# Loading q and k in runs of four tokens (1 KB), with heads 0-3 on partitions 0-63 and heads 4-7 on partitions 64-127

## The chip, the cores and the metric

The kernel runs on one core of one Trainium2 chip. The metric is device time in microseconds of one execution; a kernel's time is the median of its fast executions. The profile's span runs from the first to the last recorded instruction, so it is a little shorter than the device time (302.3 us where 304.1 us was timed for the same run). Some executions fall into a slower state with a lower TensorE clock; they are marked and left out of every comparison.

## The reference, cut to what matters

The reference is attention inside chunks of 64 tokens, followed by a bilinear feed-forward block on the result. Batch is 8, heads 8, sequence 576, head size 64, all in fp32:

```python
q_c = q.reshape(B, H, nc, chunk, D)                 # chunk = 64, the same for k and v
attn = softmax(np.matmul(q_c, k_c.transpose(0, 1, 2, 4, 3)) / sqrt(D))
out = np.matmul(attn, v_c)
x = out.transpose(0, 2, 1, 3).reshape(4608, 512)    # tokens x (heads * head size)
return (x @ w_a) * (x @ w_b) @ w_out                # w_a, w_b: 512 x 1536, w_out: 1536 x 512
```

## The kernel before

It works on units of 256 tokens (18 units). A unit that crosses from one batch into the next is loaded in two pieces. For the first units (q of units 0 to 5, k of units 0 to 4) q and k are transposed on TensorE; later ones are transposed by DMA. The change touches only those first units. These are the parts concerned:

```python
# load: two tokens to a partition, so each of the 8 heads brings a run of 512 B
st = st_pool.tile([128, H, 2, D], FP32, name="st")
for r, b, s, m in pieces(U):
    nc.sync.dma_start(
        out=st[r // 2:(r + m) // 2].rearrange("p h i d -> p h (i d)"),
        in_=src[b, :, s:s + m, :].rearrange("h (p i) d -> p h (i d)", i=2),
    )
staged[n, U] = st.rearrange("p h i d -> p i h d")
...
# transpose_pe: 8 transposes into PSUM, then two copies that interleave the tokens again
for i in range(2):
    for m in range(NKT):
        nc.tensor.transpose(tp[i][:, m, :],
            src[:, i, 2 * m:2 * m + 2, :].rearrange("p j d -> p (j d)"), identity)
dst = qkt[U][:, w].rearrange("c g m (p i) -> c i m g p", i=2)
for i in range(2):
    on_dve = i == 0 if U == 0 else w == 0 or U == 1
    cp = nc.vector.tensor_copy if on_dve else nc.scalar.copy
    cp(out=dst[:, i], in_=tp[i].rearrange("c m (g p) -> c m g p", g=2))
```

Partition p holds tokens 2p and 2p+1, so a transpose of "token i of every partition" yields every second token, and the copy out of PSUM writes every second bf16 element (a step of two). And in unit 1, on which the head of the kernel ends, all four copies are VectorE's.

The softmax here doesn't subtract the row's maximum and nothing guards it: scores larger than these inputs give would overflow.

## Time and profile before

| | before |
|---|---|
| median (three runs, then four with one more beside the changed kernel) | 303.82 us, then 303.66 us |
| span of the profiled run | 302.3 us |
| TensorE busy | 292.4 us, 97% |
| VectorE, ScalarE, GpSimd busy | 69%, 65%, 64% |
| start of the first real matmul of the feed-forward block | 17.65 us |

The busy rows show tenths of busy time in 40 equal slices of the span. These are the four copies of unit 1 in the kernel before, from VectorE's instructions in order of time (start, duration, engine, line, operation, output and input; in brackets the idle time before it and what ended it):

```profile
9.42 0.73 DVE L240 COPY qkt<-pq 128x512 bf16<-128x512 bf16 x1 [1.22 <-PE pq L231]
10.05 0.71 DVE L240 COPY qkt<-pt 128x512 bf16<-128x512 bf16 x1
10.93 0.73 DVE L240 COPY qkt<-pb 128x512 bf16<-128x512 bf16 x1 [0.17 <-PE pb L231]
11.55 0.71 DVE L240 COPY qkt<-pa 128x512 bf16<-128x512 bf16 x1
```

Two of them had to wait for transposes (the brackets of 1.22 and 0.17). From the first copy's start to the scores at 12.32 is 2.90 us. VectorE is busy in nearly all of this stretch, so a copy that is much longer shows up in full.

### The profile page before, as it was taken

The numbers are of one execution on the slowest core, as the hardware profiler recorded it, in microseconds if no ns is written. First come the engines' busy times: TensorE is split into PE (matmuls) and PEld (weight loads), VectorE is DVE, ScalarE is ACT, GpSimd is POOL, SyncE is SP. The second block draws the span as 40 slices with busy tenths as digits, with TensorE's granted clock in tenths as the row PEclk, the third lists the DMA queues.
The fourth block names the chain that finished last, engine by engine and source line by source line (L and its number), as shares of the span: only waits on it lengthen the run. The fifth ranks groups of instructions, "written<-read, shape, count | busy, mean of one in ns | idle before, by whom it ended". The sixth has DMA issues, their size and how long they took to land.

```text
span 302.3 us, 8608 instructions
## 1 busy us (share of the span) xinstructions
PE 292.4 (97%) x3527; PEld 231.9 (77%) x3527; DVE 210.0 (69%) x343; ACT 196.5 (65%) x355; POOL 193.3 (64%) x180
## 2 busy tenths in 40 slices
PE   6799999999999999999999999999999999999995
PEld 2344367866588888888888888888888888888884
DVE  3456575878767696769676966796679667965773
ACT  2643567348387768776867687768776876566532
POOL 0665758995999698808880888178817901780660
PEclk9999999999999999999999999999999999999999
DMA  7999999999999999896959395958721001100024
GB/s 222 307 382 284 283 336 345 242 217 210 219 239 262 213 242 276 188 210 181 208 122 245 129 205 132 210 163 198 123 87 72 2 2 69 73 0 3 2 98 179
DMA packets 141127, 54.29 MB, mean 180 GB/s; under 512 B 117152, under 2 KB 135200, under 8 KB 141088
## 3 DMA queue, kind: packets, MB, share of 16 engines
q1 hardware_dynamic: 140944, 53.69, 69.9%
q8 instruction: 27, 0.44, 0.6%
q14 instruction: 12, 0.10, 0.1%
q10 hardware_dynamic: 144, 0.07, 0.1%
HBM read 37.75 MB, written 9.44 MB: 156 GB/s over the span
## 4 chain that ended last, share of the span: by engine, by line
PE 83%; DMA 5%; SPq 4%; DVE 3%; POOL 1%; ACT 1%; issue 1%; DVEq 0%; ACTq 0%; POOLq 0%
PE pb L440 19%; PE pc L440 12%; PE pa L440 12%; PE po L578 12%; PE pq L578 10%; PE pb L651 3%; DMA st<-in_k_dram 3%; DMA st<-in_moe_w_b_dram 2%; PE po L390 2%; PE pc L390 2%; PE pa L390 2%; PE pq L390 2%; PE pt L328 2%; PE pt L295 2%; SPq L112 1%; SPq L194 1%
## 5 line engine op out<-in xcount | busy, mean ns | idle before, releaser
L520 POOL TENSOR_TENSOR so<-ab_sb 128x512 f16<-128x512 f16 x23 | 27.4, 1190 | 68.5 <-DVE ab_sb L490 68.5
L440 PEld LDWEIGHTS <-t 128*128 128x128 f16 x504 | 48.3, 98 | 8.4 <-issue 1.7
L440 PE MATMUL pb<-s,wa 128*128 128x256 f16 x336 | 50.5, 273 | 0.0
L440 PE MATMUL pa<-xT,wb 128*128 128x256 f16 x336 | 50.4, 273 | 0.0
L478 DVE TENSOR_TENSOR c_sb<-pc,v_sb 128x512 f32<-128x512 f32 x42 | 28.9, 687 | 27.7 <-ACT v_sb L451 27.7
L578 PEld LDWEIGHTS <-ab_sb 128*128 128x128 f16 x390 | 37.8, 98 | 5.2 <-issue 0.9
L440 PEld LDWEIGHTS <-wb 128*128 128x128 f16 x336 | 32.9, 98 | 4.0
L440 PEld LDWEIGHTS <-wa 128*128 128x128 f16 x336 | 31.8, 98 | 4.3 <-issue 0.2
L490 DVE SCALAR_TENSOR_TENSOR ab_sb<-pc,c_sb 128x512 f16<-128x512 f32 x42 | 29.0, 690 | 7.8 <-PE pc L440 6.3
L451 ACT COPY u_sb<-pb 128x512 f32<-128x512 f32 x42 | 24.7, 588 | 14.9 <-PE pb L440 14.7
L490 DVE SCALAR_TENSOR_TENSOR ab_sb<-pb,b_sb 128x512 f16<-128x512 f32 x42 | 28.9, 689 | 6.1 <-PE pb L440 5.2
L458 ACT COPY pb<-pa 128x512 f32<-128x512 f32 x42 | 24.1, 573 | 10.3 <-PE pa L440 10.0
L578 PEld LDWEIGHTS <-so 128*128 128x128 f16 x288 | 28.1, 98 | 3.4
L451 ACT COPY b_sb<-pa 128x512 f32<-128x512 f32 x42 | 25.0, 595 | 7.1 <-PE pa L440 7.1
L479 DVE TENSOR_TENSOR pc<-pc,u_sb 128x512 f32<-128x512 f32 x42 | 28.9, 688 | 0.0
L520 POOL TENSOR_TENSOR so<-so,ab_sb 128x512 f16<-128x512 f16 x23 | 27.4, 1192 | 1.7
L451 ACT COPY v_sb<-pb 128x512 f32<-128x512 f32 x42 | 24.7, 587 | 5.1 <-PE pb L440 4.4
L520 POOL TENSOR_TENSOR ab_sb<-ab_sb 128x512 f16<-128x512 f16 x23 | 26.8, 1166 | 0.0
L520 POOL TENSOR_TENSOR so<-ab_sb,so 128x512 f16<-128x512 f16 x23 | 26.1, 1163 | 0.0
L338 DVE TENSOR_TENSOR xT<-pt,ln 128x512 f16<-128x512 f32 x29 | 18.8, 685 | 9.9 <-PE pt L328 6.5
L440 PE MATMUL pb<-s,t 128*128 128x256 f16 x168 | 25.3, 273 | 0.0
L440 PE MATMUL pc<-xT,t 128*128 128x256 f16 x168 | 25.2, 272 | 0.1
(129 smaller groups left out, 574.4 us busy)
## 6 DMA issues: line engine op xcount, KB each, us to landing
out_dram<-o_sb SPq DMA_DIRECT2D x34, 256.0 KB, 2.3
st<-in_v_dram SPq DMA_DIRECT2D x32, 256.0 KB, 4.7
st<-in_k_dram SPq DMA_DIRECT2D x25, 256.0 KB, 4.5
st<-in_q_dram SPq DMA_DIRECT2D x23, 256.0 KB, 3.7
st<-in_moe_w_b_dram SPq DMA_DIRECT2D x6, 512.0 KB, 7.1
st<-in_moe_w_a_dram SPq DMA_DIRECT2D x6, 512.0 KB, 7.0
st<-in_moe_w_out_dram SPq DMA_DIRECT2D x6, 512.0 KB, 6.4
st<-in_q_dram SPq DMA_DIRECT2D x4, 512.0 KB, 5.7
```

The source lines that it names most:

```text
L295: nc.tensor.matmul(sm[cl][j * 64:j * 64 + 64, :], ones[cl * 64:cl * 64 + 64, :], E[cl * 64:cl * 64 + 64, j].rearrange("p m g s -> p (m g s)"),
L338: nc.vector.tensor_tensor(out=x.rearrange("p m (g c s) -> p m g c s", g=2, c=2)[:, m, :, cl, :], in0=av[cl][:, m], in1=rs[:, cl, m].rearra ...
L390: nc.tensor.matmul(ps[n], w_ab[n, i][:, kt, o:o + 128], xT[:, kt, c0:c1], start=(kt == 0), stop=(kt == NKT - 1),)
L440: nc.tensor.matmul(t[:, h * 256:h * 256 + 256], w[:, kt, h * 128:h * 128 + 128], x[:, kt], start=start and h == 0 and kt == 0, stop=h == 1 ...
L451: nc.scalar.copy(out=t, in_=src)
L458: nc.scalar.copy(out=self.B, in_=self.A)
L478: nc.vector.tensor_tensor(out=self.c, in0=self.C, in1=self.v, op=ADD)
L479: nc.vector.tensor_tensor(out=self.C, in0=self.C, in1=self.u, op=ADD)
L490: nc.vector.scalar_tensor_tensor(out=self.dst[:, :, c0:c0 + 256], in0=t.rearrange("p (h n) -> p h n", h=2), scalar=AB_SCALE, in1=o.rearran ...
L520: (eng or nc.gpsimd).tensor_tensor(out=o, in0=x0, in1=x1, op=op)
L578: nc.tensor.matmul(t[:, c0:c0 + 256][:, cols], a[:, kt, th * 128:th * 128 + 128], w[:, kt, cols], start=n in (0, 4) and first and kt == 0, ...
L651: nc.tensor.matmul(out_ps[K, tg], ab_tiles[K][:, ft, tg * 128:tg * 128 + 128], wo_sb[:, ft], start=(ft == 0), stop=(ft == NFT - 1),)
```

## The change

The intent is longer runs in DRAM. Four tokens go to a partition, so a run is 1 KB instead of 512 B. With four tokens to a partition 256 tokens fill only 64 partitions, so heads 0-3 go to the lower 64 and heads 4-7 to the upper 64, each by a transfer of its own. The bytes are the same, the packets fewer. The diff, cut to its core:

```diff
-                st = st_pool.tile([128, H, 2, D], FP32, name="st")
+                st = st_pool.tile([128, 4, 4, D], FP32, name="st")
                 for r, b, s, m in pieces(U):
-                    nc.sync.dma_start(
-                        out=st[r // 2:(r + m) // 2].rearrange("p h i d -> p h (i d)"),
-                        in_=src[b, :, s:s + m, :].rearrange("h (p i) d -> p h (i d)", i=2),
-                    )
+                    for o in range(2):
+                        nc.sync.dma_start(
+                            out=st[64 * o + r // 4:64 * o + (r + m) // 4].rearrange(
+                                "p h i d -> p h (i d)"
+                            ),
+                            in_=src[b, 4 * o:4 * o + 4, s:s + m, :].rearrange(
+                                "h (p i) d -> p h (i d)", i=4
+                            ),
+                        )
 ... (views of the cast, of the transposed tile and of the scores' operands follow)
-            dst = qkt[U][:, w].rearrange("c g m (p i) -> c i m g p", i=2)
+            dst = qkt_tile(U)[:, w].rearrange("c (o m q i) -> c i m o q", o=2, m=2, i=4)
             for i in range(2):
 ...
-                cp(out=dst[:, i], in_=tp[i].rearrange("c m (g p) -> c m g p", g=2))
+                cp(
+                    out=dst[:, 2 * i:2 * i + 2],
+                    in_=tp[i].rearrange("c (i m o q) -> c i m o q", i=2, m=2, o=2),
+                )
```

The instruction counts on the four compute engines stay. The copy keeps its 512 elements per partition, but its innermost loop (the index q of the pattern, not the tensor q) now writes every fourth bf16 element.

More of the change, by code (lines that the diff above doesn't have):

```diff
@@ L212, in cast, with qkt_tile, qkt_view @@
             eng = nc.vector if U == 0 and n != "v" else nc.gpsimd
-            eng.tensor_copy(out=raw[n, U], in_=staged.pop((n, U)))
-    qkt = {}
+            dst = raw[n, U]
+            if U < PE_UNITS[n]:
+                dst = dst.rearrange("p a (b h) d -> p (a b) h d", b=2)
+                raw[n, U] = dst
+            eng.tensor_copy(out=dst, in_=staged.pop((n, U)))
+    qkt = {}
+    def qkt_tile(U):
+        if U not in qkt:
+            qkt[U] = qkt_pool.tile([128, 2, 2 * NKT * 128], BF16, name="qkt")
+        return qkt[U]
+    def qkt_view(U, n):
+        t = qkt[U][:, "qk".index(n)]
+        if U < PE_UNITS[n]:
+            return t.rearrange("c (m g p) -> c g m p", m=NKT, g=2)
+        return t.rearrange("c (g m p) -> c g m p", g=2, m=NKT)
     def transpose_pe(U, names="qk"):
-        if U not in qkt:
-            qkt[U] = qkt_pool.tile([128, 2, 2, NKT, 128], BF16, name="qkt")
         for n in names:
@@ L225, in transpose_pe @@
             tp = [
-                t[i % len(t)].bitcast(BF16).rearrange("c (i m p) -> c i m p", i=2, m=NKT)[:, i]
+                t[i % len(t)].bitcast(BF16).rearrange("c (i n) -> c i n", i=2)[:, i]
                 for i in range(2)
             ]
-            for i in range(2):
-                for m in range(NKT):
+            for i in range(4):
+                for m in range(2):
+                    o = (i % 2) * 256 + m * 128
                     nc.tensor.transpose(
-                        tp[i][:, m, :],
+                        tp[i // 2][:, o:o + 128],
                         src[:, i, 2 * m:2 * m + 2, :].rearrange("p j d -> p (j d)"),
@@ L239, in transpose_pe @@
                 cp = nc.vector.tensor_copy if on_dve else nc.scalar.copy
-                cp(out=dst[:, i], in_=tp[i].rearrange("c m (g p) -> c m g p", g=2))
+                cp(
+                    out=dst[:, 2 * i:2 * i + 2],
+                    in_=tp[i].rearrange("c (i m o q) -> c i m o q", i=2, m=2, o=2),
+                )
     def transpose_dma(U):
-        if U not in qkt:
-            qkt[U] = qkt_pool.tile([128, 2, 2, NKT, 128], BF16, name="qkt")
-        for w, n in ((0, "q"), (1, "k")):
+        for n in "qk":
             if U < PE_UNITS[n]:
                 continue
+            qkt_tile(U)
             nc.sync.dma_start_transpose(
-                out=qkt[U][:, w].rearrange("p g m c -> p (g m) c"),
+                out=qkt_view(U, n).rearrange("p g m c -> p (g m) c"),
                 in_=raw.pop((n, U)).rearrange("p g h d -> p (g h d)"),
@@ L260, in scores @@
     def scores(U, pools=(None, None), now=2):
-        t = qkt.pop(U)
+        qt, kt = qkt_view(U, "q"), qkt_view(U, "k")
+        qkt.pop(U)
         E_of[U] = sm_pool.tile([128, 2, NKT, 2, 64], BF16, name="E")
@@ L269, in scores @@
                             sc[j][cl * 64:cl * 64 + 64, m, g, :],
-                            t[j * 64:j * 64 + 64, 1, g, m, cl * 64:cl * 64 + 64],
-                            t[j * 64:j * 64 + 64, 0, g, m, cl * 64:cl * 64 + 64],
+                            kt[j * 64:j * 64 + 64, g, m, cl * 64:cl * 64 + 64],
+                            qt[j * 64:j * 64 + 64, g, m, cl * 64:cl * 64 + 64],
                             start=m == 0 and g == 0,
```

## The prediction

> **What bounds the kernel now.** I read the busy rows of the page first, then the stretches of the head, then the instructions in order of time, then who waited for whom. The page says that TensorE is the bound nearly everywhere and that the DMA engines are full for the first half:
>
> ```profile
> PE   6799999999999999999999999999999999999995
> DMA  7999999999999999896959395958721001100024
> ```
>
> Only the first two of the 40 slices (7.56 us each) and the last have an idle TensorE. The stretches confirm it: of 0 to 17.6 us TensorE is busy 12.61 us, part of it dummy matmuls that keep it warm; of 80 to 290 us it is busy 209.86 of 210 us. So the change can pay or cost in the head, where TensorE waits for loads, and nearly nowhere else. The head, by VectorE and GpSimd in order of time (start, duration, engine, line, what; in brackets the idle time and its releaser):
>
> ```profile
> 4.78 0.69 DVE L213 CAST q_raw<-st 128x1024 bf16<-128x1024 f32 x1 [3.57 <-DMA st<-in_q_dram]
> 6.26 0.69 DVE L213 CAST k_raw<-st 128x1024 bf16<-128x1024 f32 x1 [0.79 <-DMA st<-in_k_dram]
> ...
> 7.89 1.04 POOL L213 CAST q_raw<-st 128x1024 bf16<-128x1024 f32 x1 [6.59 <-DMA st<-in_q_dram]
> 9.39 1.04 POOL L213 CAST k_raw<-st 128x1024 bf16<-128x1024 f32 x1 [0.47 <-DMA st<-in_k_dram]
> ```
>
> Every cast starts when its load lands, and loads land 1.48, 1.63 and 1.50 us apart, in a row, for 512 KB each: the DMA engines set the pace. From the cast of k of unit 1 (9.39) a fixed chain runs: transposes, copies, scores (12.32), exponentials and logarithms on ScalarE without a break from 12.81 to 17.14, the last multiply on VectorE, then the first real matmul:
>
> ```profile
> 17.65 1.02 PE L390 MATMUL pb<-xT,wb 128*128 128x512 f16 x4 [0.24 <-DVE xT L338]
> ```
>
> From there TensorE runs almost without a gap. One more place waits for loads, at 30 to 34 us:
>
> ```profile
> 28.43 1.04 POOL L213 CAST q_raw<-st 128x1024 bf16<-128x1024 f32 x1 [1.25 <-DMA st<-in_q_dram]
> 30.66 1.27 POOL L213 CAST k_raw<-st 128x1024 bf16<-128x1024 f32 x1 [1.19 <-DMA st<-in_k_dram]
> ...
> PE pb L390 <- POOL wb L120: 0.4, 1, 0.4
> PE pc L390 <- POOL wa L120: 0.2, 1, 0.2
> ```
>
> k of unit 2 lands late, the two weight casts queue behind it on GpSimd, and TensorE waits 0.4 and 0.2 us for them. There is no slack at that point.
>
> The loads at stake, at the rate at which they move (last column GB/s; the stretches are q and k of units 0 and 1; weights; q and k of unit 2; then unit 3, and unit 4 with what follows it):
>
> ```profile
> 3.00:8.50 5.50, 3.70 (x28) 1.51 (x30) 2.63 (x4) 1.46 (x2) 0.61 (x1) 1.00 1.14 346
> 15.50:23.50 8.00, 7.74 (x67) 3.50 (x66) 4.29 (x9) 3.36 (x6) 5.39 (x6) 1.00 1.09 385
> 24.50:27.50 3.00, 3.00 (x15) 1.37 (x14) 1.98 (x4) 0.74 (x2) 1.56 (x2) 1.00 1.24 244
> ...
> 51.00:54.50 3.50, 3.50 (x61) 2.88 (x59) 2.14 (x5) 2.50 (x7) 3.50 (x4) 1.00 1.22 245
> 37.70:40.20 2.50, 2.50 (x46) 1.21 (x43) 1.61 (x2) 2.37 (x4) 1.56 (x2) 1.00 1.14 344
> ```
>
> This is the view that decides. Runs of 512 B to all 128 partitions move at 346 and 344 GB/s, runs of 1 KB (weights, 128 partitions) at 385. But the same runs of 512 B move at only 244 and 245 GB/s where a unit crosses from one batch into the next, so that the load is cut into one transfer for partitions 0-31 and one for 32-127 (unit 2), or 0-63 and 64-127 (unit 4). Those are the only plain loads of q and k that do not span all partitions, and they are the slow ones, with the engines shown just as busy.
>
> **What the Trainium skill says.** "SBUF — State Buffer", Door 1: The DMA port swizzle: partitions 0-63 reach only 8 of the 16 ports through which DMA writes, 64-127 the other 8; 1 MiB moved at 196 GB/s to 64 partitions and 328 to 128. The trace agrees in direction: 244 against 346. The same page, "Can I just issue two DMAs to hit both halves?": no, two transfers to the two halves gained only 6% over one, because they go through the same DMA engines one after the other. Unit 4 is exactly that case, and its 245 GB/s is nearer to half speed than to full. "DMA: Bandwidth & Descriptors", Why small descriptors are slow: a fixed overhead for each packet, which longer runs spread. The trace agrees: 293 GB/s with v's 256 B at 8.7 to 10 us, 346 with 512 B, 385 with 1 KB. That is the gain that the change is after.
>
> **The change part by part.** The order of instructions shows equal counts on TensorE, VectorE, ScalarE and GpSimd, in the same order: 8 transposes for each tensor and unit, the same casts of 128x1024, the same PSUM copies of 128x512 (now written with a step of four elements instead of two). I take these at their old durations, 0.72 us a copy: no difference. SyncE issues 30 loads of q and k instead of 15 (8 pieces of q, 7 of k, each doubled). An issue that is not held up took 0.45 us (the first of all), so two halves cost some 0.9 us of issue for 512 KB, less than the transfer takes: hidden, except that the second half of the very first q goes out 0.5 us later, still before the first half has moved.
>
> What changes is the transfer. Intended: 1 KB runs at 385 instead of 346 GB/s, 524,288 B in 1.36 instead of 1.52 us, 0.15 us less for each of four loads, **0.6 us** in the head. Expected instead: each half reaches half of the ports. I take 240 GB/s, between the measured 245 and a little less (twice 8 ports one after the other; the longer run does not help a port that is full): 524,288 / 240 = 2.18 us, 0.67 us more for each. Four loads precede the chain: 4 x 0.67 = **2.7 us**. All later loads of the head (v and the first weights) stand behind them in the same queue and move by the same amount, so the first real matmul goes from 17.65 to about 20.3 us.
>
> Unit 2: its transfers of 32 and 96 partitions become four of 16, 16, 48 and 48 partitions. Sixteen partitions reach still fewer ports, but such short transfers may overlap with the next. By the measured 244 GB/s q took 2.15 us; I estimate 2.6, so 0.45 us each for q and k, **0.9 us** together, in full on TensorE because there was no slack. Unit 3 gets 0.67 us later for q and again for k, but its casts wait for other things (0.6 us for TensorE, 0.5 for VectorE) and the PE transposes come about a microsecond after the casts: **0.3 us** at most. Unit 4 was cut already. q of unit 5 is cast at 63.0 and transposed at 68.05: hidden. GpSimd, full from 50 to 70 us, starts that stretch later, but q of unit 4 has 5 us between cast (56.0) and transposes (62.3). Sum: 2.7 + 0.9 + 0.3 = 3.9 us; 303.8 + 3.9 = **307.7 us**.
>
> **The rivals.** (a) Two halves close behind each other overlap in the DMA engines, both sets of ports work, and the longer runs win: -0.6 us in the head and some tenths at unit 2, 302.9 us. For it: the queue holds many transfers, and one half is only 16 KB for each engine. Against it: unit 4 had the same 16 KB for each engine and half, and moved at 245. (b) Worse than taken: pieces of 16 and 48 partitions run one after the other on few ports; q and k of unit 2 then cost up to 1.4 us more each instead of 0.45, and TensorE idles so long in the head that its clock falls ("TensorE: Matmul & The Clock Gate", Why this matters: no idle gaps above about 3 us; the trace has none that long in the head, and the gaps grow by 0.7). That makes 310 to 311 us. (c) The number of transfers in flight becomes the bound: the built program has eight completion counters for loads, and each issue waits for the transfer eight before it. With halves, eight are 2 MB in the head, 1 MB at unit 2; at 240 GB/s that is 4 us of work at unit 2, about the landing time of a single transfer in the page's list (3.7 to 4.7 us for 256 KB), so I expect at most some tenths, inside (b).
>
> **Range and chances.** The rate of a half decides: 250 GB/s gives 2.3 us in the head, 220 gives 3.5; unit 2 gives 0 to 2.8. The low end of the range, 305.0, is a good overlap at unit 2 with 2 us in the head or less; the high end, 310.0, is both terms near their worst. Rival (a) gets about one chance in ten and stays within 2% anyway. 2% slower begins at 309.9 us: chance 0.12. 2% faster would need 297.7, more than all that the head could give: 0.01. Within 2%: 0.87.
>
> **What would show it.** Step 1: the casts of q, k, q, k at 4.78 to 9.39 come 2.2 us apart instead of 1.5, and the rate from 3 to 11 us is near 240 GB/s; if it is 385, rival (a) holds. Step 2: the first L390 matmul (another line number there) starts at 20.3. Step 3: TensorE waits over 1 us between it and the scores of unit 2, at the transposes or the weights. Step 4: from 60 us on the kernel is the old one, shifted; durations of casts, copies and transposes are unchanged. The prediction is wrong if the halves overlap, or if the PSUM copies with the wider step take longer than 0.72 us, which would delay the chain of the head as well.

## The result, and the profile after

The changed kernel took **312.36 us** (median of four, 311.55 to 313.35) against 303.66 us (303.34 to 304.27). The ratio is 1.0286, with a 95% interval of 1.0250 to 1.0321: **slower**. Ratios here are the mean time of one kernel's fast runs over that of the other's of the same rounds, so they are not quite the ratio of the medians. The two profiled runs have spans of 309.8 and 302.3 us, 7.5 us apart.

The page of the changed kernel, with the busy tenths of TensorE and of the DMA engines:

```profile
PE   6679988998999999999999999999999999999995
DMA  7999999899999999997849685969342101200025
```

As before, TensorE is full after the start. The first ten slices have more gaps, and that is where to look. The packets became fewer, as intended; this is before:

```profile
DMA packets 141127, 54.29 MB, mean 180 GB/s; under 512 B 117152, under 2 KB 135200, under 8 KB 141088
```

and this after:

```profile
DMA packets 135735, 54.30 MB, mean 175 GB/s; under 512 B 117392, under 2 KB 129808, under 8 KB 135696
```

There are 5,392 fewer packets for the same bytes. (The means of 180 and 175 GB/s are over the whole span; the longer span alone makes the second one lower, so the loads have to be judged by stretches.) The stretches of the changed kernel that answer to those of the prediction are q and k of units 0 and 1; weights; and q and k of unit 2. Columns are the length, busy time and count for TensorE, its weight loads, VectorE, ScalarE and GpSimd, the granted clock, the DMA share and, last, GB/s:

```profile
3.00:10.00 7.00, 4.62 (x24) 2.26 (x22) 2.75 (x4) 1.53 (x2) 0.00 (x0) 1.00 1.08 259
19.00:26.00 7.00, 6.77 (x60) 2.93 (x60) 3.34 (x6) 3.80 (x7) 4.64 (x5) 1.00 1.08 381
26.50:29.00 2.50, 2.50 (x13) 1.14 (x12) 1.47 (x3) 0.59 (x1) 1.10 (x2) 1.00 1.15 236
```

The weights, to 128 partitions, kept their rate (385 before, 381 now). The loads by halves of the head fell from 346 to 259 GB/s, and that is the prediction's first step. The head of the changed kernel on VectorE, in order of time:

```profile
5.45 0.69 DVE L222 CAST q_raw<-st 128x1024 bf16<-128x1024 f32 x1 [4.25 <-DMA st<-in_q_dram]
7.95 0.69 DVE L222 CAST k_raw<-st 128x1024 bf16<-128x1024 f32 x1 [1.80 <-DMA st<-in_k_dram]
...
12.36 1.30 DVE L261 COPY qkt<-pq 128x512 bf16<-128x512 bf16 x1 [1.36 <-PE pq L252]
13.47 1.36 DVE L261 COPY qkt<-pt 128x512 bf16<-128x512 bf16 x1
14.61 1.36 DVE L261 COPY qkt<-pb 128x512 bf16<-128x512 bf16 x1
15.75 1.35 DVE L261 COPY qkt<-pa 128x512 bf16<-128x512 bf16 x1
```

and on GpSimd:

```profile
10.05 1.04 POOL L222 CAST q_raw<-st 128x1024 bf16<-128x1024 f32 x1 [8.74 <-DMA st<-in_q_dram]
12.22 1.04 POOL L222 CAST k_raw<-st 128x1024 bf16<-128x1024 f32 x1 [1.13 <-DMA st<-in_k_dram]
```

The casts are now 2.50, 2.10 and 2.17 us apart instead of about 1.5, so k of unit 1 is cast 2.83 us later (12.22 against 9.39). And every copy takes 1.30 to 1.36 us instead of 0.71 to 0.73. VectorE runs the four without a pause, and the scores wait for the last of them. This is the longest of TensorE's waits in the first 48 us of the changed kernel (what waited, for what; total, times, longest in us):

```profile
PE po L292 <- DVE qkt L261: 2.2, 1, 2.2
```

Before, the same wait was this:

```profile
PE po L268 <- DVE qkt L240: 0.5, 1, 0.5
```

The first real matmul answers to 17.65 of before:

```profile
23.10 1.02 PE L414 MATMUL pb<-xT,wb 128*128 128x512 f16 x4
```

The head can be added up from these starts:

| step of the head | before | after | later by |
|---|---|---|---|
| first copy of unit 1 starts | 9.42 | 12.36 | 2.94 |
| from there to the scores of unit 1 | 2.90 (to 12.32) | 4.80 (to 17.16) | 1.90 |
| from there to the first real matmul | 5.33 (to 17.65) | 5.94 (to 23.10) | 0.61 |
| sum | | | 5.45 |

The first row is mostly loads: in e1 below, with the slow loads and the old copies, the same copy starts at 11.63. The other 0.73 us come from the slow copies of unit 0, because TensorE takes the scores of unit 0, which wait for them, before it transposes q of unit 1. The second row is copies. The third I come back to with the clock (e9).

The rest came later and was not in the prediction. Between 40 and 76 us TensorE waited for these in the changed kernel:

```profile
PE pt L292 <- ACT qkt L261: 0.8, 1, 0.8
PE pa L292 <- ACT qkt L261: 0.8, 1, 0.8
PE pq L414 <- ACT u_sb L422: 0.4, 1, 0.4
PE pc L414 <- DVE ab_sb L423: 0.4, 1, 0.4
```

The kernel before has none of these four in the same part of its work; its longest wait there is 0.2 us. The first two are the scores of units 4 and 2, waiting for slow copies that are ScalarE's in those units. The other two are evacuations of the feed-forward block, which stand behind the copies on the same engines.

I matched the two traces' matmuls in order and took the difference of their starts. Such shifts, at five matmuls of the kernel before, are used below:

| kernel, changed minus before, us | unit 1, k transposed (10.49) | unit 1, scores (12.32) | first real matmul (17.65) | weights after unit 2's loads (34.15) | unit 4, scores (64.9) | last |
|---|---|---|---|---|---|---|
| the change | +2.83 | +4.84 | +5.46 | +4.52 | +7.39 | +7.55 |
| e1, halves alone | +2.73 | +2.98 | +3.87 | +3.14 | +4.05 | +4.26 |
| e2, wide step alone | -0.21 | +2.55 | +3.30 | +2.36 | +5.23 | +5.59 |
| e11, change with mended copies | +2.89 | +3.14 | +3.33 | +2.93 | +3.39 | +3.73 |
| e6, change with mended partitions | +1.64 | +4.40 | +5.00 | +4.06 | +6.90 | +7.14 |
| e7, both mended | +1.39 | +1.35 | +1.39 | +1.92 | +2.42 | +2.44 |
| e12, both mended, units 0 and 1 only | +1.27 | +1.52 | +1.71 | +0.84 | +0.85 | +0.82 |
| e10, twice the transfers alone | +1.09 | +1.54 | +1.54 | +0.97 | +1.46 | +1.39 |

### The profile page after: what moved, and what is told of

Same layout as the page of the kernel before. It is cut to its first block, busy times and chain, and to the rows that moved or that the text cites. A ratio compares the mean times of both kernels' runs of the same rounds, so it can differ in the third digit from the quotient of the medians.

```text
span 309.8 us, 8632 instructions
## 1 busy us (share of the span) xinstructions
PE 295.3 (95%) x3525; PEld 234.1 (76%) x3527; DVE 216.8 (70%) x343; ACT 201.2 (65%) x355; POOL 193.3 (62%) x180
## 4 chain that ended last, share of the span: by engine, by line
PE 81%; DMA 7%; DVE 4%; POOL 3%; SPq 2%; ACT 1%; issue 1%; POOLq 0%; DVEq 0%
PE pb L464 18%; PE pc L464 12%; PE pa L464 12%; PE po L602 12%; PE pq L602 9%; DMA st<-in_moe_w_out_dram 3%; PE pb L414 3%; DMA st<-in_k_dram 2%; PE po L414 2%; PE pt L352 2%; DVE qkt L261 2%; PE pc L414 2%; SPq L182 1%; PE pt L319 1%; POOL wot L164 1%
```

## The experiments

My theory after the comparison had two causes. The halves slow the loads, as predicted, and the copies with a step of four take 1.3 us, which the prediction had ruled out. The rivals: the order of the copy's dimensions rather than its step; 64 partitions being slow as such, rather than which 64; the TensorE clock; and the number of transfers. All kernels gave correct results. All times are in us, and the medians are of fast runs alone: one run of four of e5 (342.14), one of six of e7 (311.27) and one of six of e8 (338.33) were slow and are left out.

| run | median | before | ratio (95% interval) |
|---|---|---|---|
| the change | 312.36 | 303.66 | 1.0286 (1.0250 to 1.0321) |
| e1_halves_only | 308.50 | 304.36 | 1.0131 (1.0113 to 1.0149) |
| e2_step4_only | 310.01 | 304.36 | 1.0186 (1.0168 to 1.0205) |
| e5_pair_copies | 308.05 | 304.09 | 1.0129 (1.0102 to 1.0156) |
| e11_pair_copies_again | 308.47 | 304.24 | 1.0138 (1.0109 to 1.0167) |
| e6_even_odd_loads | 311.60 | 304.09 | 1.0254 (1.0230 to 1.0277) |
| e7_both_mended | 306.45 | 304.09 | 1.0103 (1.0065 to 1.0141) |
| e12_mended_units01 | 305.47 | 304.24 | 1.0047 (1.0027 to 1.0068) |
| e8_before_pair_copies | 304.05 | 304.09 | 0.9997 (0.9980 to 1.0015) |
| e9_more_warm | 311.76 | 304.90 | 1.0243 (1.0196 to 1.0290) |
| e10_two_by_heads | 306.17 | 304.90 | 1.0045 (0.9998 to 1.0091) |

### e1: the halves alone

The kernel before, with its loads cut at partition 64. Runs stay at 512 B and the copies stay as they were.

```diff
-                    nc.sync.dma_start(
-                        out=st[r // 2:(r + m) // 2]...,
+                    cuts = [r, 128, r + m] if r < 128 < r + m else [r, r + m]
+                    for c, e in zip(cuts, cuts[1:]):
+                        nc.sync.dma_start(out=st[c // 2:e // 2]..., in_=src[b, :, s + c - r:s + e - r, :]...)
```

> The kernel before, with each load of q and k for the PE transposes cut at partition 64 into two transfers, still with runs of 512 B; the copies out of PSUM are the old ones. Theory (two costs that add: halves of the partitions load slowly, and the PSUM copies that write every fourth bf16 element take 1.3 instead of 0.72 us): loads land 2.2 us apart instead of 1.5, the first real matmul starts about 2.8 us later (20.4 us), copies stay at 0.72 us, and the whole is 3 to 4.5 us slower than before (306.7 to 308.2 us). Rival (the loads are nearly the whole loss and the slow copies are hidden): 311 to 312 us. Rival (the slow loads are hidden, copies are all): 304 us.

It took 4.14 us more than the kernel before (308.50 against 304.36), where the prediction gave the loads 3.9. The copies kept their 0.71 to 0.73 us. So the loads, with what follows from them, explain somewhat under half of the change's 8.7 us. That their total was predicted so well is partly luck (see the end).

### e2: the wide step alone

The kernel before, loads untouched. The transposed q and k of units 0 to 4 are interleaved, q and k in turn, so that a copy writes every fourth element instead of every second. Its dimensions keep their order.

```diff
-            dst = qkt[U][:, w].rearrange("c g m (p i) -> c i m g p", i=2)
+            if U < 5:
+                dst = qkt[U].rearrange("c w g m p -> c (w g m p)").rearrange(
+                    "c (g m p i w) -> c w i m g p", g=2, m=NKT, i=2, w=2)[:, w]
+            else:
+                dst = qkt[U][:, w].rearrange("c g m (p i) -> c i m g p", i=2)
```

The matmuls of the scores then read every second element. They are no slower for it: their median is 193 ns in this kernel and before.

> The kernel before, its loads untouched; for units 0 to 4 the PSUM copies write every fourth bf16 element (q and k interleaved in one tile, the matmuls read every second element; the result stays right). The copies keep the old order of dimensions. Theory (the step of 8 bytes is what slows the copies): each copy takes about 1.3 us instead of 0.72, the first real matmul starts about 2 us later (19.7 us), the whole is 3 to 5 us slower (306.8 to 308.8 us). Rival (the extra dimension or the order of dimensions in the changed kernel's copies slows them, not the step): copies stay at 0.72 us and the time at 304 us.

It took 5.65 us more (310.01 against 304.36), and the scores of unit 1 waited as in the changed kernel, longer still because k was there on time. The longest of TensorE's waits in this kernel:

```profile
PE po L282 <- DVE qkt L245: 3.6, 1, 3.6
```

So the step by itself costs more than the halves. The table of shifts tells where: 2.55 us before the scores of unit 1, and 2.87 us between the weights after unit 2 and the scores of unit 4 (2.36 to 5.23). The changed kernel has the same 2.87 us there (4.52 to 7.39). The two causes by themselves add up to 9.8 us against 8.7 us together, so in part they hide each other.

### e3: the copies by themselves

The kernel before, with twelve copies each on VectorE and ScalarE added after its work, all from the same PSUM tile. A single run; its time says nothing, only the durations do.

```diff
+            eng(out=y[:, 0:512], in_=x)                       # step 1
+            eng(out=y[:, 0:1024:2], in_=x)                    # step 2
+            eng(out=y[:, 0:1536:3], in_=x)                    # step 3
+            eng(out=y[:, 0:2048:4], in_=x)                    # step 4
+            eng(out=v4[:, 0:2].rearrange("c i m o q -> c m o q i"),   # the change's elements, pair innermost
+                in_=x5.rearrange("c i m o q -> c m o q i"))
 ... (and the patterns of both kernels, four dimensions at step 2, 256 elements at steps 4 and 8)
```

> The kernel before with twelve copies of bf16 from PSUM to SBUF on VectorE and twelve on ScalarE after all its work, with write steps of 1, 2, 3, 4 and 8 elements and with the dimensions of both kernels. Theory (step): 512 elements take about 0.72 us at steps 1 and 2 in any order of dimensions, and about 1.3 us at step 4 in any order; step 3 and 8 tell where the limit lies. Rival (dimensions): the pattern of the changed kernel is slow at step 2 as well, and a flat step of 4 is fast. The whole is some 12 us longer, which says nothing.

VectorE in order of time, six of the twelve (steps 1, 2, 3, 4, then the changed kernel's own pattern, then its elements in the other order):

```profile
300.58 0.42 DVE L956 COPY st<-pt 128x512 bf16<-128x512 bf16 x1
301.04 0.73 DVE L957 COPY st<-pt 128x512 bf16<-128x512 bf16 x1
...
303.32 1.01 DVE L960 COPY st<-pt 128x512 bf16<-128x512 bf16 x1
304.36 1.29 DVE L961 COPY st<-pt 128x512 bf16<-128x512 bf16 x1
...
307.01 1.29 DVE L963 COPY st<-pt 128x512 bf16<-128x512 bf16 x1
...
310.42 0.69 DVE L966 COPY st<-pt 128x512 bf16<-128x512 bf16 x1
```

Each further element of step adds 0.28 to 0.31 us. A plain step of four takes as long as the changed kernel's pattern with its many dimensions, and four dimensions at step two took 0.72 us, so the number of dimensions is not the cause. With half the elements the times were 0.73 us at step four and 1.29 us at step eight, so what counts is the width that is written over. ScalarE gave 0.59, 0.73, 1.01 and 1.29 us for steps one to four. The last line points at the remedy. The change's copy writes elements 0 and 1 of each group of four; if the innermost loop goes over that pair, the same 512 elements take 0.69 us (0.59 on ScalarE).

### e4: the loads by themselves

The kernel before, with loads of q and k in eight forms after its work, one form after the other, four tiles of each. A single run; only the rates are read.

```diff
+        for j, (x, b) in enumerate(both):   # both: q and k of batches 0 and 1
+            for o in range(2):              # the changed kernel's form: halves, 1 KB
+                nc.sync.dma_start(out=to(64 * o, 64 * o + 64, j, 256),
+                                  in_=of(x, b, 4 * o, 4 * o + 4, 0, 256, 4))
 ... (and seven other forms)
```

> The kernel before with loads of the same kind measured by themselves after all its work, one form after the other with a stop in between, 1 to 2 MB each. Theory (partitions 0-63 reach only half of the write ports, 64-127 the other half): 128 partitions at 512 B 345 GB/s and at 1 KB 385; halves 0-63 and 64-127 about 240 to 260 at both run lengths; partitions 32-95 alone, which have all ports, clearly faster than 0-63 alone (300 or more against 220 at most); 16 and 48 partitions 200 to 230. Rival (a transfer of 64 partitions or of 256 KB is slow as such): 32-95 alone is as slow as 0-63 alone. The whole is some 60 us longer, which says nothing.

The stretches in which each form moved, last column GB/s. In order: 128 partitions with 512 B; halves with 512 B; halves with 1 KB; partitions 32-95 alone; partitions 0-63 alone; 128 partitions with 1 KB; even and odd partitions in turn, 1 KB; and pieces of 16, 16, 48 and 48 partitions, as in unit 2 of the change:

```profile
304.00:308.00 4.00, 0.00 (x0) 0.00 (x0) 0.51 (x3) 0.00 (x0) 0.00 (x0) 0.50 1.15 347
309.00:315.00 6.00, 0.00 (x0) 0.00 (x0) 0.51 (x3) 0.00 (x0) 0.00 (x0) 0.50 1.22 255
317.00:324.00 7.00, 0.00 (x0) 0.00 (x0) 0.68 (x4) 0.00 (x0) 0.00 (x0) 0.50 1.11 255
325.40:326.40 1.00, 0.00 (x0) 0.00 (x0) 0.34 (x2) 0.00 (x0) 0.00 (x0) 0.50 1.08 372
331.50:333.80 2.30, 0.00 (x0) 0.00 (x0) 0.34 (x2) 0.00 (x0) 0.00 (x0) 0.50 1.07 203
335.00:339.00 4.00, 0.00 (x0) 0.00 (x0) 0.62 (x4) 0.00 (x0) 0.00 (x0) 0.50 1.09 385
340.50:344.50 4.00, 0.00 (x0) 0.00 (x0) 0.51 (x3) 0.00 (x0) 0.00 (x0) 0.50 1.09 383
346.00:353.00 7.00, 0.00 (x0) 0.00 (x0) 0.51 (x3) 0.00 (x0) 0.00 (x0) 0.50 1.13 203
```

The fourth and fifth lines decide. Both are 64 partitions with 1 KB runs; partitions 32-95 move at 372 GB/s and partitions 0-63 at 203. (The first of these rates is read over one microsecond only, since the forms follow each other closely; the landings bear it out: the first three tiles of partitions 32-95 landed 0.6 us apart, those of partitions 0-63 1.25 to 1.8 us.) So it matters which partitions, not how many, and the rival that 64 partitions are slow as such falls. This is what the table of ports in "SBUF — State Buffer", Door 1: The DMA port swizzle, of the Trainium skill leads one to expect: partitions 32-95 take half of each 64, and by the table they reach all 16 ports. Even and odd partitions, each a transfer of 64, get the full 383. And lines two and three show that 1 KB instead of 512 B gains nothing once the halves limit the rate (255 both times).

### e5 and e11: the change with its copies mended

One edit to the changed kernel: the innermost loop of the copy goes over the pair.

```diff
-                    out=dst[:, 2 * i:2 * i + 2],
-                    in_=tp[i].rearrange("c (i m o q) -> c i m o q", i=2, m=2, o=2),
+                    out=dst[:, 2 * i:2 * i + 2].rearrange("c i m o q -> c m o q i"),
+                    in_=tp[i].rearrange("c (i m o q) -> c m o q i", i=2, m=2, o=2),
```

> The changed kernel with one thing undone: the same PSUM copies write the same elements, but with the token of the pair as the innermost dimension, so two neighbouring elements follow each other and PSUM is read with a step instead. Loads stay in halves. Theory (loads and copies add): copies take 0.69 us on VectorE and 0.59 on ScalarE as measured by themselves, loads still land 2.2 us apart, the whole is 307.5 to 308.7 us, as with the halves alone (308.5), against 312.4 changed. Rival (the copies cost little where they stand): 311 us or more.

The fast runs gave a ratio of 1.0129. The same kernel again:

> The same kernel as the pair-copies run (the change with its copies writing pairs innermost), repeated because that profile fell in the slow state. Copy theory: copies near 0.69 us on VectorE and 0.59 on ScalarE, casts of the head where the changed kernel had them (k of unit 1 near 12.2), and the first real matmul near 21.4 to 21.7 us (23.10 less the 1.9 us that the slow copies added between k's cast of unit 1 and the scores, allowing for some slow TensorE clock); timed 307.5 to 308.7. Rival, the remaining cost is the slow loads alone: then it equals the halves-only run, 4.1 us over the kernel before; if it is 1 us or more above that, something else is left.

The ratio was 1.0138. The copies took 0.68 to 0.69 us on VectorE and 0.59 on ScalarE, and k of unit 1 was still cast late (12.28). The first real matmul came at 20.98 us, a little earlier than expected, against 23.10 in the changed kernel. By the shifts, mended copies take 2.1 us out of the head (5.46 to 3.33) and most of the later loss (2.87 to 0.46 us between the weights after unit 2 and the scores of unit 4). The ratio falls from 1.0286 to 1.0138, some 4.5 us of 304. What remains is at the level of e1 (1.0131): the slow loads and what follows from them; the runs show nothing else.

### e6: the change with its partitions mended, slow copies kept

Heads 0-3 go to the even partitions and heads 4-7 to the odd ones.

```diff
-                            out=st[64 * o + r // 4:64 * o + (r + m) // 4]...
+                            out=st[o + r // 2:o + (r + m) // 2 - 1:2]...
 ...
-                    in_=tp[i].rearrange("c (i m o q) -> c i m o q", i=2, m=2, o=2),
+                    in_=tp[i].rearrange("c (i m q o) -> c i m o q", i=2, m=2, o=2),
```

> The changed kernel with the other thing undone: heads 0-3 go to the even partitions and heads 4-7 to the odd ones, so each transfer still has 64 partitions and 1 KB runs but all partitions' ports. The copies keep the step of four. Theory: loads of a whole unit land 1.35 to 1.4 us apart (385 GB/s, measured by itself in this form), copies stay at 1.3 us, the whole is 308.5 to 310 us, like the step of four alone (310.0), less the faster loads. Rival (64 partitions or the doubled number of transfers is what is slow): loads 2.2 us apart and 312 us.

A miss: 311.60, a ratio of 1.0254 whose interval overlaps the change's. The loads did become faster (k of unit 1 cast at 10.56 instead of 12.22), yet the scores came only 0.4 us earlier. VectorE in order of time shows why:

```profile
11.95 1.30 DVE L261 COPY qkt<-pq 128x512 bf16<-128x512 bf16 x1 [1.37 <-PE pq L252]
13.05 1.34 DVE L261 COPY qkt<-pt 128x512 bf16<-128x512 bf16 x1
```

The copies of unit 1 start at 11.95 and then run back to back, as in the changed kernel. What held their start are slow copies too: q of unit 1 was cast at 8.90, but TensorE first takes the scores of unit 0, which waited until 10.73 for unit 0's copies, so q was transposed at 11.30 only. Once the copies bind the end of the head, k of unit 1 may land 1.7 us earlier without effect. I had subtracted the gain of one cause as if the other did not stand behind it.

### e7 and e12: both mended

The edits of e5 and e6 together.

> The changed kernel with both mended: 1 KB runs to even and odd partitions, and copies that write pairs. Theory: loads 0.15 us faster each than in the kernel before and copies no slower, so the head ends 0.6 to 0.9 us earlier and the whole is 302.5 to 303.7 us, against 304.0 before. Rival (something else in the change costs, for example twice the number of transfers with eight in flight): above 304.5 us.

Another miss: 306.45, 2.36 us over the kernel before. The head was nearly mended: the first real matmul came at 19.04 instead of 23.10. But the loads did not reach the 383 GB/s of e4. Here are the head and the loads of unit 2:

```profile
3.00:9.00 6.00, 3.63 (x23) 1.88 (x22) 2.42 (x4) 0.59 (x2) 0.00 (x0) 0.91 0.96 310
27.00:30.00 3.00, 3.00 (x16) 1.34 (x15) 1.97 (x5) 1.17 (x2) 1.50 (x2) 1.00 0.59 156
```

The column before GB/s is the DMA share. At unit 2 it is 0.59: the engines have nothing to move. The waits of the DMA queue name the reason:

```profile
SPq L195 <- DMA st<-in_moe_w_a_dram: 1.7, 1, 1.7
SPq L195 <- DMA st<-in_moe_w_b_dram: 0.8, 1, 0.8
```

and TensorE waits for a weight cast (GpSimd's) right after unit 2, longer than the 0.4 and 0.2 us of before:

```profile
PE pc L414 <- POOL wa L120: 1.2, 1, 1.2
```

Two of the four pieces of k of unit 2 go out only when a weight load issued eight loads earlier has landed. The kernel before has no such wait. This is the prediction's rival (c), the eight completion counters, which twice as many transfers use up twice as fast. To see how much of the loss sits there I kept the mended form for units 0 and 1 alone and loaded and copied units 2 to 5 exactly as before:

```diff
+            if 2 <= U < PE_UNITS[n]:
+                ... (the load, the transposes and the copies of the kernel before)
```

> Even and odd partitions, 1 KB runs and pair copies for units 0 and 1 alone; units 2 to 5 loaded and copied exactly as in the kernel before. Theory that the doubled count costs both in the head and at unit 2: the head as in the both-mended run (first real matmul near 19.0, 1.4 later than before), unit 2's weight matmuls no later than that, no wait for loads of eight before ahead of k of unit 2, and timed 1.0 to 1.7 us over the kernel before instead of 2.6. Rival, all of the both-mended run's loss is in the head: the two are within 0.4 us. Rival, the loss is all at unit 2: this one is within 0.4 us of the kernel before.

It took 1.23 us more than the kernel before instead of 2.36, and the wait for loads of eight before is gone. In the shifts, the weights after unit 2 are 0.84 us late instead of 1.92 and nothing is added afterwards. So about half of e7's remainder comes from how it handles units 2 to 5, and half is in the head. (By the runs alone the intervals of e7 and e12 just touch; the shifts are what separates them.) That the wait for loads of eight before is what costs at unit 2 is not shown: e12 also undoes the form of the loads and the copies there, and e10 below has nearly the same two waits without such a loss.

### e10: twice the transfers alone

The kernel before, each load cut in two by heads. Both transfers go to all partitions, runs are 512 B and the copies are as before.

```diff
+                    for o in range(2):
+                        nc.sync.dma_start(
+                            out=st[r // 2:(r + m) // 2, 4 * o:4 * o + 4]...,
+                            in_=src[b, 4 * o:4 * o + 4, s:s + m, :]...)
```

> The kernel before with each load of q and k for the PE transposes cut in two by heads: twice as many transfers, as in the changed kernel, but each to all of the unit's partitions, runs of 512 B. It prices the number of transfers by itself. The version with both mended was at 306.6 and not at the 303 I expected. Theory A (the number of transfers costs, with eight in flight and a slower issue): DMA runs dry near 28 us as it does there, the time is 305 to 307 us. Theory B (what is left in the mended version comes from even and odd partitions colliding at the ports when the first transfers start): the time is 303.8 to 304.5 us, loads 1.5 us apart.

The runs leave it open whether it is slower (1.0045, with 1 in the interval). The trace shows a later head: the first real matmul at 19.19 instead of 17.65. Two stretches of it:

```profile
4.00:6.50 2.50, 2.29 (x12) 0.88 (x9) 0.69 (x1) 0.36 (x1) 0.00 (x0) 1.00 0.93 251
7.00:8.50 1.50, 0.34 (x4) 0.34 (x5) 1.09 (x2) 0.00 (x0) 0.00 (x0) 1.00 1.14 343
```

From 4 to 6.5 us the rate is low with the DMA share at 0.93; from 7 us on it is the 343 GB/s of before. So the doubled count costs something at the very start, and e12 shows about the same size there. One trace alone would be weak evidence: between the changed kernel and e9, whose loads are the same, k of unit 1 is cast 0.94 us apart. But in all four kernels that double the transfers while each still spans both halves of the partitions (e6, e7, e10, e12) it is cast at 10.48 to 10.78, against 9.39 before and 9.19 in e2. Why the engines are not full in these microseconds, with transfers in the queue, stays open. In the changed kernel this is part of what the halves cost: e1 has the doubled count too.

At unit 2 the doubled count by itself shows no loss. The queue's waits for the load eight before are there,

```profile
SPq L195 <- DMA st<-in_moe_w_a_dram: 1.8, 1, 1.8
SPq L195 <- DMA st<-in_moe_w_b_dram: 0.6, 1, 0.6
```

but the shift falls from 1.54 to 0.97 there, as in e12 (1.71 to 0.84), while it rises in e7 (1.39 to 1.92). So e7's loss at unit 2 needs more than these waits; what, stays open.

### e8: does the kernel before gain from the better order of copies?

The kernel before, its transposes regrouped so that a PSUM tile holds both tokens of two head pairs, and the copy writes without gaps.

```diff
-            dst = qkt[U][:, w].rearrange("c g m (p i) -> c i m g p", i=2)
+            dst = qkt[U][:, w].rearrange("c g m (p i) -> c m g p i", i=2)
```

> The kernel before with copies that write runs without a step (both tokens of a pair in one PSUM bank, read with a step). Copies 0.69 us on VectorE and 0.59 on ScalarE instead of 0.72 and 0.73; four of those on VectorE stand in the chain of the head, so I expect 0.1 to 0.3 us less, 303.7 to 304.2 us, hardly to be told from the kernel before.

The ratio is 0.9997 (0.9980 to 1.0015): no gain. No kernel beats the one before.

### e9: the TensorE clock

The head of the changed kernel ran 0.61 us longer between the scores and the first real matmul, and TensorE seemed to run slowly there. The clock column of the view reads 1.00, but the dummy matmuls that keep it warm took 0.38 us in the kernel before and these 0.61 us in the changed one:

```profile
18.16 0.61 PE L101 MATMUL pc<-warm_in 128*128 128x512 bf16 x1
```

So I added more dummies in the waits:

```diff
-        keep_warm(8)
+        keep_warm(11)
 ...
-        transpose_pe(1)
+        transpose_pe(1, "q")
+        keep_warm(2)
+        transpose_pe(1, "k")
 ...
-        keep_warm(1)
+        keep_warm(6)
```

> The changed kernel with more dummy matmuls in the waits of the head (11 instead of 8 before the first transposes, 3 for 1, 4 for 2, 2 for none, 6 for 1). In the changed kernel a dummy of 512 columns takes 0.61 to 0.63 us from 7 to 20 us, against 0.38 in the kernel before: TensorE's clock has fallen in the longer waits. Theory (the slow clock adds 0.6 us at the end of the head, the rest of the loss is loads and copies): dummies at 0.38 us from about 7 us on, the first real matmul at 22.3 to 22.7 us instead of 23.1, the whole 0.4 to 1 us less than the changed kernel, 311.3 to 312 us. Rival (the clock is the main part of the loss over the predicted 307.7): 309 us or less.

The dummies are fast again:

```profile
18.37 0.39 PE L101 MATMUL pc<-warm_in 128*128 128x512 bf16 x1
```

The first real matmul came at 23.03 instead of 23.10, and the intervals of this run and of the change overlap. That does not clear the clock, though. In this execution k of unit 1 was cast at 13.16 instead of 12.22, with the same loads, so the scores came at 17.70 instead of 17.16. From there to the first real matmul it took 5.33 us, as in the kernel before, instead of 5.94. So the 0.61 us are TensorE running slowly, and the later load hid the gain. The other traces agree: this stretch takes 5.33 to 5.37 us in the kernel before, e7, e9 and e10, where all its dummies take 0.38 to 0.39 us; 5.52 in e11 and e12; and 5.93 to 6.22 in the change, e1, e2 and e6, where the first two or more take 0.61 to 0.63. The time, 311.76, lies in the expected range but is not told apart from the change's: how much of the 0.61 us reaches the end of the kernel is not shown.

The 1.00 of the clock column is no measurement here: the changed kernel's trace has no clock record before 20.64 us, and the view then prints 1.00. Where this run has records, they agree with its dummies, which took 0.63 us from 10.05 to 11.34 us and 0.38 from 12.93 on (the column before DMA share and GB/s):

```profile
9.10:12.40 3.30, 3.17 (x44) 1.79 (x44) 2.44 (x3) 1.33 (x1) 1.04 (x1) 0.50 1.21 237
12.50:23.00 10.50, 8.18 (x144) 3.97 (x141) 7.17 (x9) 6.44 (x11) 6.25 (x6) 1.00 1.01 305
```

Nor had the changed kernel's clock "fallen in the longer waits", as the expectation has it: its dummies are slow from the first one at 1.26 us on, and none is fast before 20.7. In the kernel before they are fast from 5.98 on.

## Why the prediction was wrong, point by point

- **What bounds the kernel: right.** Nearly all of the loss arises in the first 70 us, where the loads set the pace of the head, as predicted, and the copies its end, which was not.
- **Halves reach half of the ports: right, and the size nearly so, partly by luck.** k of unit 1 was cast 2.83 us later, against 2.7 us predicted; the casts are 2.1 to 2.5 us apart, and the rate of the head is 259 GB/s against 240. The rival (a), overlap of the halves, does not hold. Part of the 2.83 us is not ports, though: at the 255 GB/s of e4 four loads take some 2.2 us longer than at 346 (an estimate), and e10 shows +1.09 us at the same point from the doubled count, which the prediction took as hidden. (Of the load rates shown in the prediction, the 245 of 51 to 54.5 us is unit 4 and the 344 of 37.7 to 40.2 is unit 3; its text names them the other way round, but reads them rightly.)
- **Unit 2, 0.9 us: wrong in size.** TensorE did not lose there. Between the first real matmul and the weights after unit 2 the shift fell from 5.46 to 4.52, and from 3.87 to 3.14 in e1. The term "in full on TensorE because there was no slack" failed, and with it step 3: TensorE itself came late from the head, and its waits of 0.4 and 0.2 us for weights at this place are gone.
- **Unit 3, 0.3 us "at most": too small.** In e1 the shift rises by 0.91 us (3.14 to 4.05) at the transposes of k of unit 3, which wait for its cast.
- **Sum of the loads, 3.9 us: right in total, by luck in part.** e1 measures 4.14 us. But its first real matmul came at 21.52, not 20.3: between the scores of unit 1 and it, 0.89 us were lost to the slow TensorE, which the sum did not count. This and unit 3's excess make up for unit 2, where nothing was lost and 0.73 us were regained.
- **"I take these at their old durations, 0.72 us a copy: no difference": this is the step that failed.** The copies took 1.30 to 1.41 us. e2 shows 5.65 us for the wider step by itself, e3 that the step and not the dimensions makes the duration, and e5 and e11 that the change with the same elements in another order is at the level of e1. The prediction had named this among the things that would make it wrong, and still gave it no share of the range. An estimate would have been at hand: the four copies of unit 1 stand on VectorE, nearly back to back, directly ahead of the scores.
- **Step 4 of "what would show it", the kernel merely shifted from 60 us on: nearly.** From unit 4's scores on the shift grows by only 0.16 us. What was missed lies between 34 and 65 us, where slow copies on ScalarE and VectorE delay scores and evacuations: 2.87 us, the same in the change and in e2.
- **Rival (b): half of it was seen.** TensorE did run slowly in the head and lost 0.61 us there (0.89 in e1), though with no wait of 3 us in the change (the longest is 2.2). The pieces of 16 and 48 partitions did move at only 203 GB/s by themselves (e4), yet unit 2 cost nothing.
- **Rival (c): the mechanism exists, its cost is not shown.** The queue does wait for the load eight before, in the changed kernel (up to 2.1 us), in e7 and in e10. Only e7 loses time at unit 2 (some 1.1 us more than e12), and e10, with the same waits, does not.

In all, of some 8.7 us the copies carry about 4.5 (1.0286 to 1.0138 when they are mended) and the loads with their doubled count the other 4.2. The 0.6 us of slow TensorE in the head are inside these two numbers.

## What to carry to other kernels

A change of a load's layout ends in the instruction that puts the elements back in order: take the step of that write from the access pattern, and look for a measured duration of the same step before calling the cost unchanged. Choose the innermost loop so that neighbouring elements are written one after the other. Split a transfer so that each part still spans both halves of the partitions (even and odd rather than lower and upper: 383 against 255 GB/s in e4), count how many transfers the split puts in flight, and don't subtract two gains on the same path as if each were alone.

## What the Trainium skill lacked or had wrong

- "SBUF — State Buffer", Door 1: The DMA port swizzle, says of SBUF's cachelines: "So how far you can stride for free depends on dtype: 4 fp32, 8 bf16, 16 int8." For bf16 copies from PSUM to SBUF this did not hold: 512 elements took 0.42, 0.73, 1.01 and 1.29 us on VectorE at steps of one to four, and 0.59, 0.73, 1.01 and 1.29 us on ScalarE. The same elements with pairs innermost took 0.69 and 0.59 us.
- The same page, "Can I just issue two DMAs to hit both halves?", gives two transfers to the two halves +6% over one, and says that one transfer over all 128 partitions is the only way to hit all 16 ports. Here halves in turn moved at 255 GB/s against 203 for one half alone, +26%, and transfers of 64 partitions that span both halves (32-95, or every second partition) moved at 372 and 383 GB/s, next to 385 for 128. The page's own table of ports agrees with those.
- I found no page that prices the number of transfers in a queue that is full: cutting each load in two, all partitions kept, delayed the first real matmul by 1.54 us in the trace (timed 1.0045, not told apart from no change). k of unit 1 was cast 1.09 us later there.
- "TensorE: Matmul & The Clock Gate", Why this matters, warns of idle gaps above some 3 us. Shorter ones went with a drop here: in e9 the granted clock reads 1.00 from 5.7 to 9.0 us and 0.50 from 9.1 to 12.4, and in e7 1.00 from 4.5 to 7.8 and 0.50 from 7.9 to 11.2, while TensorE's longest wait up to there was 1.7 and 1.6 us. (Elsewhere the page does say that frequent short idle times made the clock of another kernel go up and down.) More dummies gave full clock from 12.5 us on in e9.
